# Dynamic convolution and SwiGLU: blocks 2 to 5 one at a time, with one queue of convolution steps, before the pairs begin

## The chip, the cores and the metric

One core of a Trainium2 chip. The metric is the time of one execution on the device in microseconds (us); shown is the median of several runs. The profile is one further execution, with the hardware profiler on. The engines are called PE (TensorE, matmuls), PEld (its weight loads), DVE (VectorE), ACT (ScalarE), POOL (GpSimd) and SP (SyncE, which issues the DMAs here). L301 is line 301 of the kernel before.

## The reference, cut to what matters

The input x is 4 x 4096 x 192. A causal convolution of 7 taps whose weights differ for every position and for each of 8 heads (24 channels a head) comes first, the weights through a softmax over the taps. Then a SwiGLU layer: RMS norm, two products with 192 x 1536 matrices, silu of the one times the other, and a product with a 1536 x 192 matrix.

```
w = exp(weight_gen - max over k); w = w / (sum over k + 1e-9)
x[b,s,h,:] = sum over k of w[b,s,h,k] * x_pad[b,s+k,h,:]
xn  = x / sqrt(mean(x*x) + 1e-6) * rms_g
out = (silu(xn @ w_gate) * (xn @ w_val)) @ w_out
```

The results are float32. The kernel gets there with float16 matmuls by splitting each operand into a high and a low float16 part.

## The kernel before, in words

The 16384 tokens are 32 **blocks** of 512 tokens (128 partitions x 4). Four blocks share one load of x and of the convolution's weights, a **group** (`load_x`, `load_w`; two buffers each). For each block i:

- **Convolution** (`conv`, L174): 13 steps on DVE, a product for each of the 7 taps (L193) and 6 additions (L204). A group's first block needs the group's softmax (`softmax`, L154), six steps on DVE and ACT.
- **Getting ready**: four squares with their sums on ACT (L209), the scale `rs` on DVE and its power -1/2 on POOL (L213, L217), the scaled block `xn` on DVE (L232), its float16 high part `sp` on ACT (L239), the low part on POOL (L241). Then `trans` (L249): SP issues a transposing DMA into `tt` (L253) and two copies with the halves swapped into `tu` (L256, L257). `tt` and `tu` have two buffers each.
- **Stage 1**: 12 chunks c of 128 hidden columns (`s1_mm`, L292). Each chunk is 18 matmuls into two PSUM banks, `pg` and `pv`; the first ones need `tt` alone, the others `tu`. The chunk is evacuated (`s1_evac`, L309) by a silu on ACT, `sg` (L314), and a product on DVE, `hf` (L316); then split (`s1_split`, L320) into the high part on ACT (L324) and the low part on POOL (L326), both in `hh`. The split runs two chunks behind, in the list `pend` (LAG = 2).
- **Stage 2**: the output product. For each of 4 tiles t of 128 tokens the 12 chunks are summed into one bank `po`, in 12 units of 4 chunks (`s2_mm`, L334; `unit`, L661). A finished tile is evacuated (`s2_evac`, L348) by ACT, `lo` (L353), and DVE, `ot` (L354); the fourth one sends the block out.

PSUM has eight banks, given out in turn (`ps1`).

The order on PE, DVE and ACT is written out by the program; POOL's and SP's in the main part is left to the framework. The start (the string START, run by `go`) brings in the weights and does blocks 0 and 1 whole, all of the convolution of block 2, and the first 4 of 13 steps for block 3 (LEAD). The main loop (L770) then takes blocks in **pairs** from block 2 on: stage 1 of block a, stage 1 of a + 1, stage 2 of a, stage 2 of a + 1.

Beside these stages run the steps that prepare later blocks. They wait in the list `work` as pairs of a cost and a function: 1.0 for a convolution step, 1.0 to 1.5 for a softmax step on DVE, 0.2 and 0.8 for `rs` and `xn`, and 0.0 for what is done on other engines. `begin` (L746) adds steps and sets a rate, at most 0.62 a slot in stage 1 and 0.88 in stage 2, and no more than spreads what is in the list over the stage's 24 slots. A slot is a chunk in stage 1 and a unit in stage 2. `beside` (L755) is called once a slot, behind that slot's matmuls and ahead of its evacuation: it adds the rate to an allowance and issues steps until the allowance is used up; steps of cost 0 follow at once. `first(a)` and `second(a)` (L632, L645) give the steps beside stage 1 and stage 2 of the pair a: `mix` (L593) gives convolution steps, `weigh` (L605) softmax steps, and `ready` (L616) what comes behind the last convolution step, with up to three steps of another list mixed in. If a block is not ready when its stage 1 is to be written out, the loop issues steps until it is (L773).

Of the kernel before, what the change touches and what calls it, by code (L numbers as in the profile page):

```python
# [20 lines left out]
J = 4  # L21
# [25 lines left out]
def tile_dynamic_conv_swiglu(  # L47
# [15 lines left out]
    NC = F // P  # L63
# [3 lines left out]
    SUB = R // J  # L67
    NB = NG * SUB
# [53 lines left out]
    def load_x(g):  # L122
        t0 = g * GT
        xt = p_x.tile([P, R + HALO, D], F32, tag="xg", name="xg")
        if t0 % S == 0:
            nc.vector.memset(xt[0:1, 0:HALO, :], 0.0)
            for a, b in ((1, 16), (16, P)):
                src = xf[t0 + a * R - HALO : t0 + b * R - HALO]
                nc.sync.dma_start(
                    out=xt[a:b, 0:HALO, :],  # L130
                    in_=src.rearrange("(p j) d -> p j d", j=R)[:, 0:HALO, :],
                )
        else:
            src = xf[t0 - HALO : t0 - HALO + GT]
            nc.sync.dma_start(
                out=xt[:, 0:HALO, :],
                in_=src.rearrange("(p j) d -> p j d", j=R)[:, 0:HALO, :],
            )
        xg[g] = xt
        load_x_slots(g, 0, J if g == 0 else R)  # L140

    def load_x_slots(g, a, b):
        src = xf[g * GT : (g + 1) * GT].rearrange("(p j) d -> p j d", j=R)
        nc.sync.dma_start(out=xg[g][:, HALO + a : HALO + b, :], in_=src[:, a:b, :])

    def load_w(g, a=0, b=R):
        if a == 0:
            wg[g] = p_w.tile([P, R, H, K], F32, tag="wt", name="wt")
        src = wf[g * GT : (g + 1) * GT].rearrange("(p j) c -> p j c", j=R)
        dst = wg[g].rearrange("p j h k -> p j (h k)")  # L150
        nc.sync.dma_start(out=dst[:, a:b, :], in_=src[:, a:b, :])
# [95 lines left out]
    xT = {}  # L247
# [44 lines left out]
    def s1_mm(i, c):  # L292
        f = slice(c * P, (c + 1) * P)
        pairs[i, c] = [ps1.tile([P, TB], F32, tag="pr", name=n) for n in ("pg", "pv")]
        orders = (OF_TT + OF_TU, OF_TU + OF_TT)
        for n in range(9):
            for m, pt in enumerate(pairs[i, c]):
                h = slice(m * L, (m + 1) * L)
                grp, wpart, xpart = orders[m][n]
                half, q = PLACE[grp, xpart]  # L300
                mm = nc.tensor.matmul(  # L301
                    pt, wm[h, grp, wpart, f], xT[i][half != m][h, q], start=(n == 0), stop=(n == 8)
                )
        return mm
# [4 lines left out]
    def s1_evac(i, c):  # L309
        pg, pv = pairs.pop((i, c))  # L310
        k = next(k for k, (a, b) in enumerate(SL) if a <= c < b)
        sg = p_e.tile([P, TB], F32, tag="sg", name="sg")
        o = 3 * k + 2 * SL[k][0]
        yield nc.scalar.activation(out=sg, in_=pg, func=AF.Silu, scale=isc[:, o : o + 1])  # L314
        hf_of[i, c] = p_e.tile([P, TB], F32, tag="hf", name="hf")
        yield nc.vector.scalar_tensor_tensor(  # L316
            out=hf_of[i, c], in0=pv, scalar=cs1[:, c : c + 1], in1=sg, op0=ALU.mult, op1=ALU.mult
        )

    def s1_split(i, c):  # L320
        if c == 0:
            hid[i] = p_h.tile([P, 2, NC, TB], F16, tag="hh", name="hh")
        hf = hf_of.pop((i, c))
        yield nc.scalar.activation(out=hid[i][:, 0, c, :], in_=hf, func=AF.Copy)  # L324
        low = nc.vector if i < 2 else nc.gpsimd
        yield low.tensor_tensor(  # L326
            out=hid[i][:, 1, c, :], in0=hf, in1=hid[i][:, 0, c, :], op=ALU.subtract
        )
# [5 lines left out]
    def s2_mm(i, t, c0, c1):  # L334
        if c0 == 0:
            po[i, t] = ps1.tile([P, 2 * D], F32, tag="pr", name="po")
        pt = po[i, t]
        c = slice(t * P, (t + 1) * P)
        for n in range(c0, c1):
            mm = nc.tensor.matmul(  # L340
                pt, hid[i][:, 0, n, c], wo[:, n, :], start=(n == 0), stop=False,
            )
            nc.tensor.matmul(  # L343
                pt[:, 0:D], hid[i][:, 1, n, c], wo[:, n, 0:D], start=False, stop=(n == NC - 1),
            )
        return mm

    def s2_evac(i, t):  # L348
        if t == 0:
            ot[i] = p_o.tile([P, J, D], F32, tag="ot", name="ot")  # L350
        pt = po.pop((i, t))
        lo = p_o.tile([P, D], F32, tag="lo", name="lo")
        yield nc.scalar.activation(out=lo, in_=pt[:, D:], func=AF.Identity, scale=so[:, 1:2])  # L353
        nc.vector.scalar_tensor_tensor(  # L354
            out=ot[i][:, t, :], in0=pt[:, 0:D], scalar=so[:, 1:2], in1=lo,
            op0=ALU.mult, op1=ALU.add,
        )
        g, s = divmod(i, SUB)
        if i == NB - 1:
            nc.sync.dma_start(out=outg[g, :, s * J + t, :], in_=ot[i][:, t, :])  # L360
        elif t == J - 1:
            nc.sync.dma_start(out=outg[g, :, s * J : (s + 1) * J, :], in_=ot.pop(i))
        yield
# [187 lines left out]
    def run(gen):  # L551
        for _ in gen:
            pass
# [39 lines left out]
    def mix(i, n):  # L593

        if i not in convs:
            convs[i] = conv(i)
        for _ in range(n):
            if begun.get(i, 0) < 2 * K - 1:
                begun[i] = begun.get(i, 0) + 1
                yield 1.0, lambda: next(convs[i])  # L600
# [4 lines left out]
    def weigh(g, steps):  # L605

        if g >= NG:
            return
        for n in steps:
            if n == 0:  # L610
                mixing[g] = softmax(g, 0, R)
            yield (1.0, 1.5, 0.0, 1.1, 1.3, 1.5)[n], lambda: next(mixing[g])
            if n == 5:
                yield 0.0, lambda: next(mixing[g], None)

    def ready(i, more):  # L616

        step = lambda: next(convs[i])
        for _ in range(J):
            yield 0.0, step  # L620
        for _ in range(2):
            yield from [x for x in [next(more, None)] if x]
        yield 0.2, step
        yield from [x for x in [next(more, None)] if x]
        yield 0.8, step
        for _ in range(2):
            yield 0.0, step
        yield 0.0, lambda: (next(convs[i], None), trans(i))

    whole = 2 * K - 1  # L630

    def first(a):  # L632

        if a == 2:
            more = weigh(1, range(6))
            yield from mix(3, whole)
            yield from ready(3, more)
            yield 0.0, lambda: (load_x(2), load_w(2))
            yield from more
        if a + 2 < NB:  # L640
            yield from mix(a + 2, whole)
        if a + 3 < NB:
            yield from mix(a + 3, EARLY)
# [15 lines left out]
    LAG = 2  # L659

    def unit(u):  # L661
        t, r = divmod(u, 3)
        return t, 4 * r, 4 * r + 4
# [74 lines left out]
    pend = []  # L738
# [3 lines left out]

    work, plan = [], [0.0, 0.0, 1.0]
    STAGE1, STAGE2 = 0.62, 0.88

    def begin(todo, slots, most):  # L746
        work.extend(todo)
        plan[:] = 0.0, 0.0, min(most, sum(cost for cost, _ in work) / slots)

    def do_next():  # L750
        cost, do = work.pop(0)
        do()
        plan[1] += cost

    def beside():  # L755
        plan[0] += plan[2]
        while work and (plan[1] < plan[0] or not work[0][0]):
            do_next()

    def stage2(i):  # L760
        for u in range(NC):
            s2_mm(i, *unit(u))
            beside()
            if u % 3 == 2:
                run(s2_evac(i, u // 3))

    with tc.manual_schedule(engines={
        mybir.EngineType.DVE, mybir.EngineType.PE, mybir.EngineType.Activation,
    }):
        for a in range(2, NB, 2):  # L770
            begin(first(a), 2 * NC, STAGE1)
            for i in (a, a + 1):
                while i not in xT:  # L773
                    do_next()
                for c in range(NC):
                    s1_mm(i, c)
                    if len(pend) == LAG:
                        run(s1_split(*pend.pop(0)))
                    beside()
                    run(s1_evac(i, c))  # L780
                    pend.append((i, c))
            while pend:
                run(s1_split(*pend.pop(0)))
            begin(second(a), 2 * NC, STAGE2)
            for i in (a, a + 1):
                stage2(i)
        assert not work
# [29 lines left out]
```

## Time and profile before

| | |
|---|---|
| median of 3 runs | 1233.79 us (1233.39 to 1234.16) |
| the profiled execution | 1235.56 us |
| its span, first to last instruction | 1233.8 us |
| mean granted clock of PE | 0.976 of full speed |
| busy: PE, DVE, ACT, POOL | 1171.5, 953.9, 659.8, 543.1 us |

How to read it: busy time is the time in which an engine had an instruction running. Matmuls are pipelined, so that a busy PE need not be at its peak. Shares over the whole span are averages of unlike stages; the stretch from 142 to 338 us is the one that the rows below look at.

### The profile page before, as it was taken

The numbers are of one execution on the slowest core, as the hardware profiler recorded it, in microseconds if no ns is written. First come the engines' busy times: TensorE is split into PE (matmuls) and PEld (weight loads), VectorE is DVE, ScalarE is ACT, GpSimd is POOL, SyncE is SP. The second block draws the span as 40 slices with busy tenths as digits, with TensorE's granted clock in tenths as the row PEclk, the third lists the DMA queues.
The fourth block names the chain that finished last, engine by engine and source line by source line (L and its number), as shares of the span: only waits on it lengthen the run. The fifth ranks groups of instructions, "written<-read, shape, count | busy, mean of one in ns | idle before, by whom it ended". The sixth has DMA issues, their size and how long they took to land.

```text
span 1233.8 us, 24345 instructions
## 1 busy us (share of the span) xinstructions
PE 1171.5 (95%) x10124; PEld 640.0 (52%) x10124; DVE 953.9 (77%) x1157; ACT 659.8 (53%) x1304; POOL 543.1 (44%) x460
## 2 busy tenths in 40 slices
PE   5899687969999999999999999999999999999998
PEld 3446235426455564645546464655546464554646
DVE  6998738559787888778887888878887889878531
ACT  4893642433654646465563646455563646556362
POOL 1100432343453636455463636456363645546351
PEclk8999889879899999999999999999999999999999
DMA  8602301011403040210503041110502011020300
GB/s 213 163 8 82 131 22 30 23 27 27 137 2 78 2 137 27 40 39 7 158 1 78 1 121 43 28 52 1 163 1 52 26 40 40 6 73 1 78 1 27
DMA packets 68086, 67.34 MB, mean 55 GB/s; under 512 B 52492, under 2 KB 55052, under 8 KB 67080
## 3 DMA queue, kind: packets, MB, share of 16 engines
q1 hardware_dynamic: 66872, 63.43, 19.2%
q10 hardware_dynamic: 1040, 2.36, 0.7%
q8 instruction: 79, 1.29, 0.4%
q14 instruction: 31, 0.25, 0.1%
q0 software_dynamic: 64, 0.00, 0.0%
HBM read 28.03 MB, written 12.58 MB: 33 GB/s over the span
## 4 chain that ended last, share of the span: by engine, by line
PE 83%; DVE 4%; issue 4%; DMA 3%; ACT 3%; POOL 2%; SPq 0%; POOLq 0%; ACTq 0%; DVEq 0%
PE pg L301 53%; PE po L340 17%; PE po L343 8%; PE pv L301 5%; DMA tt<-sp 1%; DMA tu<-tt 1%; DVE tmp L193 1%; DMA rawa<-in_moe_w_gate_dram 1%; DVE acc L204 1%; POOL hh L326 1%; POOL sp L241 1%; POOL rs L217 1%; ACT sg L314 1%; ACT junk L209 1%; DVE hf L316 0%
## 5 line engine op out<-in xcount | busy, mean ns | idle before, releaser
L301 PEld LDWEIGHTS <-wm 64*128 64x128 f16 x6912 | 348.1, 95 | 455.6 <-DMA tt<-sp 35.8
L326 POOL TENSOR_TENSOR hh<-hf,hh 128x512 f16<-128x512 f32 x360 | 446.1, 1245 | 312.3 <-ACT hh L324 312.2
L301 PE MATMUL pg<-tt,wm 64*128 64x512 f16 x1920 | 484.6, 381 | 34.6 <-DMA tt<-sp 34.3
L301 PE MATMUL pv<-tu,wm 64*128 64x512 f16 x1920 | 483.0, 380 | 4.3 <-DMA tu<-tt 4.3
L316 DVE SCALAR_TENSOR_TENSOR hf<-pv,cs,sg 128x512 f32<-128x512 f32 x384 | 284.0, 744 | 164.3 <-ACT sg L314 164.0
L301 PE MATMUL pv<-tt,wm 64*128 64x512 f16 x1536 | 399.7, 381 | 2.8 <-DVE hf L316 1.0
L314 ACT ACTIVATE sg<-pg,isc 128x512 f32<-128x512 f32 x384 | 262.6, 685 | 259.1 <-PE pv L301 246.5
L301 PE MATMUL pg<-tu,wm 64*128 64x512 f16 x1536 | 398.0, 380 | 0.6 <-DMA tu<-tt 0.6
L340 PE MATMUL po<-wo,hh 128*128 128x384 f16 x1536 | 377.9, 326 | 0.0
L343 PE MATMUL po<-wo,hh 128*128 128x192 f16 x1536 | 376.3, 246 | 0.0
L193 DVE TENSOR_TENSOR tmp<-xg,wt 128x768 f32<-128x768 f32 x194 | 257.1, 1327 | 1.8 <-DMA xg<-in_x_dram 1.8
L324 ACT ACTIVATE hh<-hf 128x512 f16<-128x512 f32 x384 | 238.6, 622 | 33.0 <-DVE hf L316 32.9
L204 DVE TENSOR_TENSOR acc<-acc,tmp 128x768 f32<-128x768 f32 x180 | 234.5, 1303 | 1.1
L340 PEld LDWEIGHTS <-hh 128*128 128x128 f16 x1536 | 150.3, 98 | 105.4 <-issue 7.2
L217 POOL TENSOR_TENSOR rs<-rs,mhalf 128x4 f32<-128x4 f32 x32 | 41.9, 1308 | 253.2 <-DVE rs L213 253.1
L343 PEld LDWEIGHTS <-hh 128*128 128x128 f16 x1536 | 150.3, 98 | 0.0
L354 DVE SCALAR_TENSOR_TENSOR ot<-po,so,lo 128x192 f32<-128x192 f32 x128 | 52.2, 409 | 75.8 <-ACT lo L353 75.8
L353 ACT ACTIVATE lo<-po,so 128x192 f32<-128x192 f32 x128 | 51.1, 411 | 108.2 <-PE po L343 105.1
L209 ACT ACTIVATE junk<-acc 128x192 bf16<-128x192 f32 x128 | 46.0, 359 | 69.6 <-DVE acc L204 61.8
L241 POOL TENSOR_TENSOR sp<-xn,sp 128x768 f16<-128x768 f32 x29 | 48.4, 1669 | 58.7 <-ACT sp L239 58.7
L239 ACT ACTIVATE sp<-xn 128x768 f16<-128x768 f32 x30 | 25.3, 843 | 84.7 <-DVE xn L232 84.6
L232 DVE TENSOR_TENSOR xn<-acc,rs 128x768 f32<-128x768 f32 x30 | 28.7, 956 | 21.8 <-POOL rs L217 21.8
(83 smaller groups left out, 316.3 us busy)
## 6 DMA issues: line engine op xcount, KB each, us to landing
tu<-tt SPq DMA_DIRECT2D x64, 192.0 KB, 2.9
out_dram<-ot SPq DMA_DIRECT2D x31, 384.0 KB, 3.3
xg<-in_x_dram SPq DMA_DIRECT2D x7, 1536.0 KB, 9.1
wt<-in_weight_gen_dram SPq DMA_DIRECT2D x7, 448.0 KB, 9.6
wost<-in_moe_w_out_dram SPq DMA_DIRECT2D x1, 2304.0 KB, 8.9
xg<-in_x_dram SPq DMA_DIRECT2D x4, 576.0 KB, 5.9
xg<-in_x_dram SPq DMA_DIRECT2D x4, 504.0 KB, 5.2
rawa<-in_moe_w_val_dram ACTq DMA_DIRECT2D x2, 384.0 KB, 7.8
```

Of the source, the lines that this page charges most:

```text
L193: yield nc.vector.tensor_tensor(out=dst.rearrange("p j (h c) -> p (j h) c", h=H), in0=xk, in1=wk, op=ALU.mult)
L204: yield nc.vector.tensor_tensor(out=acc, in0=acc, in1=dst, op=ALU.add)
L209: yield nc.scalar.activation(out=junk, in_=acc[:, j - a, :], func=AF.Square, accum_out=ssq[:, j : j + 1])
L217: yield nc.gpsimd.tensor_tensor(out=rs, in0=rs, in1=mhalf, op=ALU.pow)
L241: yield low.tensor_tensor(out=sp[:, :, D:], in0=xn, in1=sp[:, :, 0:D], op=ALU.subtract)
L301: mm = nc.tensor.matmul(pt, wm[h, grp, wpart, f], xT[i][half != m][h, q], start=(n == 0), stop=(n == 8))
L314: yield nc.scalar.activation(out=sg, in_=pg, func=AF.Silu, scale=isc[:, o : o + 1])
L316: yield nc.vector.scalar_tensor_tensor(out=hf_of[i, c], in0=pv, scalar=cs1[:, c : c + 1], in1=sg, op0=ALU.mult, op1=ALU.mult)
L324: yield nc.scalar.activation(out=hid[i][:, 0, c, :], in_=hf, func=AF.Copy)
L326: yield low.tensor_tensor(out=hid[i][:, 1, c, :], in0=hf, in1=hid[i][:, 0, c, :], op=ALU.subtract)
L340: mm = nc.tensor.matmul(pt, hid[i][:, 0, n, c], wo[:, n, :], start=(n == 0), stop=False,)
L343: nc.tensor.matmul(pt[:, 0:D], hid[i][:, 1, n, c], wo[:, n, 0:D], start=False, stop=(n == NC - 1),)
```

## The change

Blocks 2 to 5 are taken singly: stage 1 of a block and then its stage 2 at once. Pairs begin with block 6. For the single blocks one queue, `early(7)`, holds all the steps for blocks 3 to 7 and the loads of groups 2 and 3 in order; it is never refilled, and its rate is fixed at 0.75 a slot in stage 1 and 0.88 in stage 2. Where the next block's convolution can begin, up to five of its steps are offered to `ready` as the mixed-in list. A bare block number in the queue is a mark: `beside` stops there, and lets the unused allowance go, until stage 1 of that block has been written out (`past`); it stands ahead of `ready` of block i with the number i - 2, the block whose `tt` and `tu` are used again. `early` takes up what `first(2)` did for block 3. In the single blocks, stage 2 goes by thirds of the hidden columns: units 1 to 4 are chunks 0 to 3 of tiles 0 to 3, units 5 to 8 chunks 4 to 7, units 9 to 12 chunks 8 to 11, so that four banks `po` are open together and all four tiles are evacuated in the last four units. The last two splits of stage 1 are no longer run ahead of stage 2, but behind its first two units.

```diff
@@ -629,14 +629,28 @@
 
     whole = 2 * K - 1
 
+    past = set()
+
+    def early(last):
+
+        more = weigh(1, range(6))
+        for i in range(3, last + 1):
+            yield from mix(i, whole)
+            if i > 3:
+                yield 0.0, i - 2
+            g, s = divmod(i - 3, SUB)
+            if s == 0:
+                yield from ready(i, more)
+                yield 0.0, lambda g=g: (load_x(g + 2), load_w(g + 2))
+                yield from more
+                more = weigh(g + 2, range(6))
+            else:
+                ahead = mix(i + 1, 5) if i < last else iter(())
+                yield from ready(i, ahead)
+                yield from ahead
+
     def first(a):
 
-        if a == 2:
-            more = weigh(1, range(6))
-            yield from mix(3, whole)
-            yield from ready(3, more)
-            yield 0.0, lambda: (load_x(2), load_w(2))
-            yield from more
         if a + 2 < NB:
             yield from mix(a + 2, whole)
         if a + 3 < NB:
@@ -742,6 +756,7 @@
 
     work, plan = [], [0.0, 0.0, 1.0]
     STAGE1, STAGE2 = 0.62, 0.88
+    SOLO, RATE = 6, (0.75, 0.88)
 
     def begin(todo, slots, most):
         work.extend(todo)
@@ -755,30 +770,52 @@
     def beside():
         plan[0] += plan[2]
         while work and (plan[1] < plan[0] or not work[0][0]):
+            if isinstance(work[0][1], int):
+                if work[0][1] not in past:
+                    plan[1] = max(plan[:2])
+                    break
+                work.pop(0)
+                continue
             do_next()
 
-    def stage2(i):
+    def stage1(i):
+        while i not in xT:
+            if isinstance(work[0][1], int):
+                work.pop(0)
+            else:
+                do_next()
+        for c in range(NC):
+            s1_mm(i, c)
+            if len(pend) == LAG:
+                run(s1_split(*pend.pop(0)))
+            beside()
+            run(s1_evac(i, c))
+            pend.append((i, c))
+        past.add(i)
+
+    def stage2(i, turn=False):
         for u in range(NC):
-            s2_mm(i, *unit(u))
+            t, c0, c1 = (u % J, u // J * 4, u // J * 4 + 4) if turn else unit(u)
+            s2_mm(i, t, c0, c1)
+            if pend:
+                run(s1_split(*pend.pop(0)))
             beside()
-            if u % 3 == 2:
-                run(s2_evac(i, u // 3))
+            if c1 == NC:
+                run(s2_evac(i, t))
 
     with tc.manual_schedule(engines={
         mybir.EngineType.DVE, mybir.EngineType.PE, mybir.EngineType.Activation,
     }):
-        for a in range(2, NB, 2):
+        begin(early(SOLO + 1), 1, STAGE1)
+        for i in range(2, SOLO):
+            plan[2] = RATE[0]
+            stage1(i)
+            plan[2] = RATE[1]
+            stage2(i, True)
+        for a in range(SOLO, NB, 2):
             begin(first(a), 2 * NC, STAGE1)
             for i in (a, a + 1):
-                while i not in xT:
-                    do_next()
-                for c in range(NC):
-                    s1_mm(i, c)
-                    if len(pend) == LAG:
-                        run(s1_split(*pend.pop(0)))
-                    beside()
-                    run(s1_evac(i, c))
-                    pend.append((i, c))
+                stage1(i)
             while pend:
                 run(s1_split(*pend.pop(0)))
             begin(second(a), 2 * NC, STAGE2)
```

## Rows read from the trace of the kernel before

**Rows 1.** The page: busy us (share) and instructions of PE; its clock in 40 slices.
```profile
PE 1171.5 (95%) x10124; PEld 640.0 (52%) x10124; DVE 953.9 (77%) x1157; ACT 659.8 (53%) x1304; POOL 543.1 (44%) x460
...
PEclk8999889879899999999999999999999999999999
```

**Rows 2.** Waits of PE from 119 to 340: us in total, times, longest.
```profile
PE pg L301 <- DMA tt<-sp: 34.3, 4, 13.6
PE pv L301 <- DMA tu<-tt: 4.3, 4, 1.8
```

**Rows 3.** Windows by stage: length, busy PE, PEld, DVE, ACT, POOL; clock, DMA, GB/s.
```profile
119.00:142.40 23.40, 23.40 (x218) 10.43 (x216) 17.18 (x19) 13.16 (x22) 10.88 (x10) 1.00 0.31 111
142.40:160.20 17.80, 2.41 (x11) 0.57 (x10) 7.17 (x8) 7.39 (x14) 4.44 (x4) 0.64 0.64 192
160.20:185.00 24.80, 24.76 (x209) 11.63 (x209) 11.02 (x14) 13.31 (x23) 12.26 (x11) 0.92 0.00 1
185.00:208.50 23.50, 23.48 (x192) 17.15 (x190) 21.79 (x28) 6.43 (x18) 4.61 (x4) 1.00 0.05 18
...
219.90:245.00 25.10, 25.07 (x206) 11.93 (x205) 15.12 (x15) 12.51 (x26) 9.25 (x8) 0.88 0.00 1
...
260.00:284.00 24.00, 23.92 (x207) 11.64 (x207) 17.15 (x17) 13.26 (x22) 12.09 (x11) 0.93 0.01 1
...
307.70:312.60 4.90, 1.83 (x10) 0.51 (x11) 4.69 (x8) 2.60 (x10) 0.00 (x0) 0.84 0.47 111
312.60:337.60 25.00, 24.96 (x208) 11.93 (x209) 17.39 (x20) 16.62 (x25) 13.63 (x12) 0.89 0.48 148
```

**Rows 4.** The chain of waits from 142 to 162: start, us, what.
```profile
147.71 1.02 POOL rs L217
...
148.75 0.97 DVE xn L232
...
149.74 0.85 ACT sp L239
...
150.66 1.64 POOL sp L241
...
152.32 3.71 DMA tt<-sp
...
156.09 4.10 DMA tu<-tt
```

**Rows 5.** DVE by line and form, stage 2 from 185 to 208.5: count, busy, mean ns.
```profile
L193 DVE TENSOR_TENSOR tmp<-xg,wt 128x768 f32<-128x768 f32 x8 | 7.6, 950 | 0.0
```

**Rows 6.** The same for DVE in stage 1 of block 5, 260 to 284.
```profile
L316 DVE SCALAR_TENSOR_TENSOR hf<-pv,cs,sg 128x512 f32<-128x512 f32 x11 | 8.2, 744 | 13.3 <-ACT sg L314 13.3
L204 DVE TENSOR_TENSOR acc<-acc,tmp 128x768 f32<-128x768 f32 x3 | 5.5, 1826 | 0.0
L193 DVE TENSOR_TENSOR tmp<-xg,wt 128x768 f32<-128x768 f32 x3 | 4.6, 1529 | 0.0
```

**Rows 7.** The same for POOL, 260 to 284.
```profile
L326 POOL TENSOR_TENSOR hh<-hf,hh 128x512 f16<-128x512 f32 x11 | 12.7, 1156 | 17.3 <-ACT hh L324 17.3
```

**Rows 8.** The same for ACT and DVE before block 3, 142.4 to 160.2.
```profile
L209 ACT ACTIVATE junk<-acc 128x192 bf16<-128x192 f32 x4 | 1.5, 363 | 2.3 <-DVE acc L204 2.2
...
L209 ACT ACTIVATION_READ_ACCUMULATOR junk<-acc 128x1 f32 x4 | 0.7, 186 | 0.0
...
L159 DVE TENSOR_TENSOR wt<-wt,mx 128x896 f32<-128x896 f32 x1 | 1.1, 1091 | 0.0
```

**Rows 9.** The page's costliest groups, the silu on ACT over the whole span.
```profile
L314 ACT ACTIVATE sg<-pg,isc 128x512 f32<-128x512 f32 x384 | 262.6, 685 | 259.1 <-PE pv L301 246.5
```

**Rows 10.** The chain of waits before block 4: issue of a copy, the second copy.
```profile
216.38 0.47 SPq L256
216.90 2.99 DMA tu<-tt
```

**Rows 11.** SP's issues, 513 to 520: the second copy of block 12.
```profile
519.05 0.59 SPq L257 DMA_DIRECT2D tu<-tt  x1
```

## The prediction

> **What bounds the kernel now.** I read the page first. PE is busy for 95% of the span, and the line of its clock shows dips in the first third only [rows 1]: what can be won lies there, or in less PE work. The change leaves every matmul in place, so only the holes count. The waits of PE name them: 34.3 us in four waits for the transposed block `tt`, 4.3 for the swapped copy `tu` [rows 2]. The windows by stage then show where they lie [rows 3]. Let S1(i) be stage 1 of block i, S2(i) its stage 2. At full clock S1 takes 23.4 us (first row of [rows 3]); S2 of two blocks takes 23.5, so 11.75 each. S1(2) ends at 142.4, and PE then does 2.4 us of work in 17.8 until block 3's copy lands at 160.2. The same happens before blocks 4 (until 219.9), 5 (260.0) and 6 (312.6), and after each hole S1 takes 24.0 to 25.1 instead of 23.4, because the granted clock is 0.88 to 0.93: it fell to the lower level (1.2 GHz) in the hole and came back some microseconds into the stage. From 142.4 to the end of S1(6) at 337.6 are 195.2 us; the work in them is four S1 and four S2, 4 x 23.4 + 4 x 11.75 = 140.6. **54.6 us are lost**, all in this stretch.
>
> Why block 3 is late is in the chain of waits [rows 4]: after the last convolution step come the squares, `rs` on POOL at 147.71, `xn`, `sp`, its low half on POOL, the transpose (3.71), the copy (4.10). Without the squares this is 12.5 us, with them some 15, in which PE has nothing: S1(3) is next in its order, and S2(2), whose input is complete, stands behind it.
>
> **The change, part by part.**
>
> *Order of the blocks.* With blocks 2 to 5 run singly, S2(i) stands between S1(i) and S1(i+1): 11.75 us of PE work lie where the chain of block i+1 runs. No instruction of PE is added.
>
> *Thirds.* S2 goes through c = 0..3 of all four tiles first, then 4..7, then 8..11. So it needs the last splits of S1, which are now issued behind S2's slots 1 and 2, only in its slot 9, 8 x 0.98 = 7.8 us in. Four sums are open instead of one; they take the four PSUM banks that c = 8 and 9 left, evacuated 2 slots before. Cost nothing; the cover is those 7.8 us. If the last split (of c = 11, on POOL) came later than that, PE would wait for it.
>
> *Queue.* I counted it by hand: 12 slots at 0.75 and 12 at 0.88 are 19.56 units per block. Of block 3's 13 steps 4 are done in the start; the 9 left go into slots 1-3, 5-7, 9-11 of S1(2), where the old rate of 0.62 placed 8 and the rest came behind. The marks (a block's number as a queue entry) are always passed when they are reached, as S1(i-2) lies far back.
>
> *DVE beside S1.* A conv step takes 0.95 us with POOL quiet [rows 5]; in S1 1.83 and 1.53 [rows 6], for POOL's 1.16 us products [rows 7] lie beside it. Mean 1.68. Four slots of 1.95 us then hold 3 steps and 4 `hf`: 3 x 1.68 + 4 x 0.74 = 8.0 against 7.8. DVE is at its limit, 0.2 late per four slots; four pairs of PSUM banks let it be about two slots late before PE waits. I take 0, the upper end is below. On the same rows: the Trainium skill, page "SBUF — State Buffer", section "Who interferes with whom", says that VectorE and GpSimd share a port pair as an exclusive lock and the loser is blocked for a whole instruction; the trace agrees (0.95 against up to 1.83), and it speaks against raising the rate.
>
> *Block 3.* Slot 10 of S1(2) ends at 142.4 - 2 x 1.95 = 138.5, its `hf` 1.5 later, 0.7 more for the steps before: step 9 runs from 140.7 to 142.2. ACT's order has four squares here, 1.5 + 0.7 = 2.2 [rows 8], ahead of slot 11's `sg`: 144.4. Then `sg` (0.69 [rows 9]) and `hf` (0.74) of slots 11 and 12 overlap to 146.7. The new order puts two softmax steps on DVE before `rs`: 1.1 to 147.8, the second (1.09 [rows 8]) waits for a POOL product until 148.9, so 150.0. With the durations of [rows 4]: `rs` 1.2 to 151.2, `xn` 152.1, `sp` 153.0, low half 154.7, `tt` 158.4. The copy: the second is issued 0.5 after the first and lands 2.99 later [rows 10], 3.5, so **162.0** (160.2 before: later, by the squares and the softmax). PE has done S2(2) by 154.2. S1(3) ends 24.8 after the copy, as in [rows 3]: 186.8. The loads of group 2 need only the last read of `xg`, two slots earlier, so I put nothing for them; if SP had them in front of the copy, that is rival 2.
>
> *Block 4.* Its steps fill slots 9-12 of S2(2) and 2-4, 6-8, 10-12 of S1(3), the last in the last slot: `hf` of slot 11 at 186.7, step to 188.1, squares 190.3, `sg` and `hf` of slot 12 to 191.7. Before `rs` the queue puts two steps of block 5, each behind one of POOL's last two products: 195.5. `rs` and its power behind the next step: 197.5; then `xn` 198.4, `sp` 199.3, low half 201.0, `tt` 204.8, `tu` **208.3**. S2(3) ended at 198.6. S1(4) ends 25.1 later [rows 3], 233.4.
>
> *Block 5.* Five of its steps run ahead, nine are done in S2(3), the last in slot 5 of S1(4); `xn` has slot 10, at 229.0. With a wait for POOL 230.9, `sp` 231.8, low half 234.0, `tt` 237.8, `tu` 241.3. S2(4) ends at 233.4 + 11.75 = 245.2: 3.9 to spare, **no hole**. The squares in slot 5 hold that slot's `hf` back by some 3.5 us, within the banks' reach. Block 6 has `xn` in slot 3 of S1(5), block 7 its transpose in slot 8 of S2(5): no hole. So S1(6) ends at 245.2 + 35.15 + 23.4 = 303.7.
>
> *Pairs from block 6.* The queue is empty there, so the pairs run as now with a clearer start.
>
> **Sum.** Lost up to S1(4)'s end: 233.4 - 142.4 - 2 x 35.15 = 20.7, afterwards 0. Against 54.6 the gain is 33.9 (337.6 - 303.7). The profiled execution took 1235.56 with a span of 1233.8; it stands 1.8 over the median 1233.79. So 1201.7 in its own terms, 1199.9 for the median. Ends for the unknown: if POOL's products stay out of the way of both chains, block 3 is 3 and block 4 some 4 us earlier, 1193; if every step in S1 of the chains takes 1.83, 4 later plus 2 of clock, 1206.
>
> **Rivals.**
> 1. DVE sets the pace of S1. If each step sits out a whole product, 0.95 + 1.16 = 2.11, four slots take 3 x 2.11 + 4 x 0.74 = 9.3: 1.5 late, 4.5 a block, 18 in four blocks if the banks absorb none: 1218; half absorbed, 1209. The Trainium skill's page above makes this the worst case. Against it: the mean in [rows 6] is 1.68. Chance 0.08.
> 2. Block 5 is late all the same, or block 3's copy stands behind the group's loads on SP: 4 to 6 us past its need plus 1.7 of clock (25.1 - 23.4), 1206 to 1208. For it: only 3.9 to spare. Chance 0.10.
> 3. The marks hold the queue, so the change does less than it says: each of blocks 5 to 7 keeps a hole like block 4's, 208.3 - 198.6 = 9.7 less 2 us done on `tt`: 3 x 8 more, 1224. Against it: my count. Chance 0.03.
> 4. Slower: the pairs lose their lead. Before block 12 the second copy is issued at 519.05 [rows 11] and lands 2.99 later at 522.0, where S1(12) starts at about 524.8 (337.6 + 46.8 + 2 x 70.2): 2.8 to spare. If a new phase made it 3 us late at all 12 pair starts from block 8 on, with 1.7 of clock each, that is 12 x 4.7 = 56: 1256. It decides from 2.8 us per pair start on. Against it: the pairs' code is unchanged and their queue starts emptier. Chance 0.03.
> 5. No change to be seen: the new holes eat the gain, 17 us longer each. Nothing speaks for it. 0.02.
>
> **Numbers.** Forecast 0.72 (1194 to 1206); shorter chains, 1186 to 1194, 0.02; rivals as above. 1193 to 1211 holds the forecast, rival 2 and a little of 1: 0.72 + 0.10 + 0.03, some 0.85; I leave it there because both ends of the chains' bounds lie in it. About 0.2% is what a measurement can tell from no change. Faster by more 0.95, within it 0.02, slower 0.03.
>
> **What would show it.** Right: PE's waits for `tt` and `tu` fall from four to two of each, before S1(3) and S1(4), with `tu` near 162 and 208; DVE's `hf` less than two slots late; S1(6) ends near 304; nothing new after it. Wrong: a wait of PE for `hf`, or for the low half of `hh` inside S2; a third hole before block 5; transposes of the pairs nearer to PE's start than now.

## The result, and the profile after

The changed kernel takes 1203.7 us (median of 4 runs) against 1233.6 before: 29.9 us less, a ratio of 0.977 (95% interval 0.974 to 0.980). The forecast was 1199.9, and a range of 1193 to 1211. The profiled execution took 1203.92 with a span of 1202.1. Runs differ by one to two microseconds in where stage 1 of block 2 starts (118.15 here, 119.02 before, up to 119.98 below), a difference from the start of the program that the change does not touch; stages are therefore counted from that point.

On the page after, PE is busy for 97% of the span (1165.0 us). Its clock in 40 slices, as in [rows 1]:

```profile
PEclk9999988999999999999999999999999999999999
```

The waits of PE after, from 119 to 340, as in [rows 2] (us in total, times, longest):

```profile
PE pg L301 <- DMA tt<-sp: 10.0, 2, 6.4
PE pv L301 <- DVE ot L354: 2.2, 2, 1.9
PE pv L301 <- DMA tu<-tt: 1.9, 2, 1.4
PE po L343 <- POOL hh L326: 0.8, 1, 0.8
PE pg L301 <- DMA tu<-tt: 0.4, 2, 0.2
PE po L340 <- ACT sg L314: 0.3, 1, 0.3
```

Two holes are left, as forecast, and the waits for `tt` fall from 34.3 to 10.0 us. But there are three waits that were not there before, for `ot`, for the low half of `hh` and for `sg`. The windows by stage, as in [rows 3] (length, busy PE, PEld, DVE, ACT, POOL; clock, DMA, GB/s), say where. In order: S1(2), S2(2), the hole, S1(3) from the copy's landing, S2(3), the hole, S1(4), S2(4), S1(5), S2(5), S1(6):

```profile
118.15:141.56 23.41, 23.41 (x217) 10.43 (x217) 18.68 (x19) 12.38 (x22) 10.42 (x9) 1.00 0.37 119
141.56:153.40 11.84, 11.84 (x98) 8.57 (x96) 7.97 (x9) 7.91 (x17) 6.04 (x5) 1.00 0.57 207
153.40:160.58 7.18, 2.01 (x12) 0.65 (x11) 6.91 (x10) 2.12 (x3) 0.00 (x0) 0.82 0.50 110
160.58:185.03 24.45, 24.45 (x207) 11.74 (x206) 18.80 (x19) 12.73 (x21) 10.91 (x10) 0.91 0.05 17
185.03:196.80 11.77, 11.77 (x98) 8.56 (x96) 8.25 (x9) 4.05 (x12) 5.27 (x4) 1.00 0.01 2
196.80:206.92 10.12, 3.03 (x12) 0.83 (x11) 8.46 (x11) 1.71 (x5) 2.40 (x1) 0.61 0.44 102
206.92:232.08 25.16, 25.16 (x206) 11.85 (x206) 15.13 (x17) 11.71 (x25) 12.15 (x9) 0.89 0.02 7
232.08:245.38 13.30, 12.20 (x98) 8.52 (x98) 11.39 (x11) 5.18 (x9) 8.34 (x6) 1.00 0.29 60
245.38:271.52 26.14, 23.97 (x218) 11.85 (x217) 22.33 (x29) 15.81 (x34) 15.40 (x11) 1.00 0.18 46
271.52:283.38 11.86, 11.86 (x97) 8.56 (x97) 10.67 (x11) 5.69 (x14) 8.14 (x5) 1.00 0.41 143
283.38:306.90 23.52, 23.47 (x216) 11.83 (x217) 20.70 (x28) 16.52 (x28) 15.84 (x11) 1.00 0.30 92
```

S2(2) and S2(3) take their plain length right behind their S1. The holes end at 160.6 and 206.9; with the 0.9 us by which this execution started earlier, the forecast of 162.0 and 208.3 was off by 0.5 each. There is no hole before blocks 5 and 6. Counted from the start of S1(2), block 3's copy lands at 42.4 us, against 41.2 before: it comes no earlier, and the hole before block 3 is shorter by the work of S2(2) that now lies ahead of it. Block 4's copy lands at 88.8 instead of 100.9, so there the queue counts as well as the order of the blocks; no run takes the two apart. What the forecast does not have is in two stages: S2(4) takes 13.30 instead of 11.75, S1(5) 26.14 instead of 23.4, at full clock. From the end of S1(2) to the end of S1(6) it is 165.3 us against 195.2 before: 29.9 gained where 33.9 were worked out.

The chain that makes block 3 ready, as in [rows 4], from the timelines of DVE, POOL and SP: the second softmax step, the power, `xn`, the low half, the transpose, the second copy, without the lines between them (start, length, engine, line; in brackets the idle time before, and who ended it).

```profile
146.59 1.97 DVE L159 TENSOR_TENSOR wt<-wt,mx 128x896 f32<-128x896 f32 x1
148.72 1.01 POOL L217 TENSOR_TENSOR rs<-rs,mhalf 128x4 f32<-128x4 f32 x1 [1.11 <-DVE rs L213]
149.76 0.96 DVE L232 TENSOR_TENSOR xn<-acc,rs 128x768 f32<-128x768 f32 x1 [1.12 <-POOL rs L217]
151.68 1.64 POOL L241 TENSOR_TENSOR sp<-xn,sp 128x768 f16<-128x768 f32 x1 [1.95 <-ACT sp L239]
153.34 1.45 SPq L253 DMA_TRANSPOSE tt<-sp  x1
157.58 0.59 SPq L257 DMA_DIRECT2D tu<-tt  x1
```

The softmax step that lies ahead of `rs` takes 1.97 us here, against 1.09 with POOL quiet [rows 8]: it ends 0.95 us after POOL's last product (147.61), as assumed. SP issues nothing between the transpose and the copies, so no load of the group stood in their way. DVE in S1(3) and POOL in S1(3), as in [rows 6, 7]:

```profile
L316 DVE SCALAR_TENSOR_TENSOR hf<-pv,cs,sg 128x512 f32<-128x512 f32 x11 | 8.2, 744 | 5.8 <-ACT sg L314 5.8
L193 DVE TENSOR_TENSOR tmp<-xg,wt 128x768 f32<-128x768 f32 x4 | 6.5, 1624 | 0.0
L204 DVE TENSOR_TENSOR acc<-acc,tmp 128x768 f32<-128x768 f32 x4 | 5.5, 1372 | 0.0
```
```profile
L326 POOL TENSOR_TENSOR hh<-hf,hh 128x512 f16<-128x512 f32 x10 | 11.6, 1156 | 20.8 <-ACT hh L324 20.8
```

A step takes 1.50 on the mean, less than the 1.68 at the lower rate: some of the steps start when a product is half done and wait for its rest alone (1.37 us for the step at 169.53, beside a product from 168.92 to 170.08). DVE still waits 5.8 us for `sg`, so it is not the pace, and S1(2) took its plain 23.41 at the rate of 0.75. The pairs kept their lead. The second copy of block 12 after, as in [rows 11], and the first matmul of S1(12) in the kernel before:

```profile
487.47 0.59 SPq L257 DMA_DIRECT2D tu<-tt  x1
```
```profile
526.52 0.39 PE L301 MATMUL pg<-tt,wm 64*128 64x512 f16 x1
```

With the 2.99 of [rows 10] the copy lands at 490.5; S1(12) starts at 494.9, so 4.4 us are to spare. Before it was 4.5 (526.5 - 522.0), not 2.8: the prediction had put the start at about 524.8.

Why S2(4) and S1(5) are longer is to be read on ACT. Two of its waits from 232 to 255 (us in total, times, longest):

```profile
ACT junk L209 <- DVE acc L204: 5.9, 1, 5.9
ACT sp L239 <- DVE xn L232: 4.5, 1, 4.5
```

ACT did its instructions in the order in which the program wrote them. The queue put `sp` of block 5 ahead of slot 10's `sg`; `sp` waits for `xn`, `xn` for the power on POOL, and that lies behind two of POOL's products. ACT stood 4.5 us, from 228.5 to 233.0, while the chunks of slots 10 to 12 came to wait. The last splits of block 4 came late, and PE waited in S2(4), 0.3 us for a PSUM bank that `sg` had not yet read and 0.8 for the last low half. In S2(4) the squares of block 6 then stood 5.9 us for DVE's last step, ahead of three `lo`; the `ot` that follow were late, and PE waited 1.9 us for a PSUM bank in S1(5). That was the theory for the experiments; the rival was that DVE and POOL, shutting each other out at the higher rate, are simply too slow.

### The profile page after: what moved, and what is told of

Same layout as the page of the kernel before. It is cut to its first block, busy times and chain, and to the rows that moved or that the text cites. A ratio compares the mean times of both kernels' runs of the same rounds, so it can differ in the third digit from the quotient of the medians.

```text
span 1202.1 us, 24340 instructions
## 1 busy us (share of the span) xinstructions
PE 1165.0 (97%) x10124; PEld 637.1 (53%) x10124; DVE 957.2 (80%) x1157; ACT 658.0 (55%) x1304; POOL 552.4 (46%) x460
## 4 chain that ended last, share of the span: by engine, by line
PE 76%; POOL 2%; DVE 2%; issue 1%; ACT 1%; POOLq 0%
PE pg L301 46%; PE po L340 17%; PE po L343 9%; PE pv L301 4%; POOL hh L326 2%; DVE tmp L193 1%; DVE acc L204 0%; DVE xn L232 0%; DVE ot L354 0%; DVE hf L316 0%; POOL rs L217 0%; ACT junk L209 0%; ACT sp L239 0%; POOL sp L241 0%; ACT sg L314 0%
## 5 line engine op out<-in xcount | busy, mean ns | idle before, releaser
L326 POOL TENSOR_TENSOR hh<-hf,hh 128x512 f16<-128x512 f32 x360 | 456.0, 1275 | 299.6 <-ACT hh L324 299.6
L193 DVE TENSOR_TENSOR tmp<-xg,wt 128x768 f32<-128x768 f32 x194 | 262.3, 1355 | 2.7 <-DMA xg<-in_x_dram 2.7
L217 POOL TENSOR_TENSOR rs<-rs,mhalf 128x4 f32<-128x4 f32 x32 | 41.2, 1288 | 226.2 <-DVE rs L213 226.2
```

The lines of the kernel that those rows point to most:

```text
L193: yield nc.vector.tensor_tensor(out=dst.rearrange("p j (h c) -> p (j h) c", h=H), in0=xk, in1=wk, op=ALU.mult)
L326: yield low.tensor_tensor(out=hid[i][:, 1, c, :], in0=hf, in1=hid[i][:, 0, c, :], op=ALU.subtract)
```

## The experiments

Eight kernels, each the changed kernel with an edit. The times beside each other are medians; lengths come from the profiles. The changed kernel takes 165.2 us from the start of S1(2) to that of S1(6) (118.15 to 283.38).

**ACT's order.** `ready` takes the numbers of mixed-in steps ahead of the squares, ahead of `rs`, ahead of `xn` and ahead of `sp` from a table; (0, 2, 1, 0) is what it did.

```diff
+    MIXED = {5: (1, 0, 1, 1), 6: (3, 1, 1, 1)}
...
     def ready(i, more):
         step = lambda: next(convs[i])
+        n0, n1, n2, n3 = MIXED.get(i, (0, 2, 1, 0))
+        take = lambda n: (x for _ in range(n) for x in [next(more, None)] if x)
+        yield from take(n0)
         for _ in range(J):
             yield 0.0, step
-        for _ in range(2):
-            yield from [x for x in [next(more, None)] if x]
+        yield from take(n1)
         yield 0.2, step
-        yield from [x for x in [next(more, None)] if x]
+        yield from take(n2)
         yield 0.8, step
+        yield from take(n3)
```

> The rates stay; only places in the queue change: the squares of block 5 come one slot later, its xn one slot earlier and its sp a slot behind xn, and the squares of block 6 wait until stage 1 of block 5. Theory (ACT stands at squares and sp that wait for DVE and POOL, ahead of evacuations that are ready): stage 2 of block 4 falls from 13.3 to about 12, stage 1 of block 5 from 26.1 to about 24; 1199 to 1201 us. Rival (POOL and DVE shutting each other out at this rate): both stages stay within 0.5 us, 1203.7.

Measured: 1201.39 (before, in the same set of runs, 1233.31; ratio 0.974, 0.972 to 0.976), 2.3 less than the changed kernel by the medians and just above the range that was expected. PE's waits from 119 to 340, then S2(4) and S1(5) in the windows, then, of ACT's waits from 208 to 245, the one for `xn`:

```profile
PE pg L301 <- DMA tt<-sp: 10.0, 2, 6.4
PE pv L301 <- DMA tu<-tt: 2.0, 2, 1.5
PE pg L301 <- DMA tu<-tt: 0.4, 2, 0.2
```
```profile
233.22:245.08 11.86, 11.86 (x98) 8.61 (x96) 11.76 (x11) 2.73 (x6) 7.61 (x5) 1.00 0.40 68
245.08:268.50 23.42, 23.42 (x217) 10.44 (x217) 21.04 (x28) 15.86 (x32) 16.96 (x11) 1.00 0.20 52
```
```profile
ACT sp L239 <- DVE xn L232: 1.5, 1, 1.5
```

Both stages are back at their plain length and only the waits for the DMAs are left: 161.3 us to S1(6), 3.9 less in the profiles. The wait for `acc` ahead of the squares, 5.9 us above, is gone. The rates are the same, and POOL is no faster. Its products in S2(4), in the changed kernel and here:

```profile
L326 POOL TENSOR_TENSOR hh<-hf,hh 128x512 f16<-128x512 f32 x5 | 7.8, 1582 | 0.0
```
```profile
L326 POOL TENSOR_TENSOR hh<-hf,hh 128x512 f16<-128x512 f32 x4 | 7.4, 1887 | 0.0
```

So DVE and POOL do shut each other out (1156 ns in S1(3) above), even more than in the changed kernel, and still PE no longer waits: new places in the queue were enough. In the changed kernel the five products took 0.4 us each more than in S1(3), on the same chain behind ACT; how much of PE's 0.8 us is theirs was not measured apart. The edit also has `rs` ready at 226.4 and its power at once behind it, at 226.5, where in the changed kernel the power waited from 228.2 to 230.1 behind two of POOL's products; so ACT's wait for `xn` falls from 4.5 to 1.5, and not only the place of `sp` counts.

**The chains of the two holes.** The same table, for other blocks (the rest of the edit as above):

```diff
+    MIXED = {3: (0, 0, 0, 0), 4: (0, 0, 0, 0)}
```

> Blocks 3 and 4 get ready with nothing mixed in: two softmax steps and three steps of block 5 are issued behind xn instead of ahead of it. Theory (the two holes left end with a chain on which these steps lie): the copy for block 3 lands 2 to 3 us earlier than 160.6, the one for block 4 another 3 to 4, in all 5 to 7 us less, 1197 to 1199. Rival (POOL's last products or the transposing DMA end the chain, and the steps lie beside them): within 1 us of 1203.7.

Measured: 1197.4 (ratio 0.971, 0.969 to 0.972), 6.3 less than the changed kernel. Counted from the start of S1(2), the copy for block 3 lands at about 40.3 instead of 42.4 (157.31 + 2.99 - 119.98), the one for block 4 at 82.7 instead of 88.8. The windows S2(2), S1(3), S2(3) with what is left of the hole, S1(4), S1(5):

```profile
143.39:159.85 16.46, 13.71 (x98) 9.43 (x97) 11.47 (x14) 8.03 (x17) 6.89 (x5) 0.90 0.61 194
159.85:183.27 23.42, 23.42 (x218) 10.44 (x217) 21.84 (x25) 14.88 (x24) 10.94 (x10) 1.00 0.05 18
183.27:202.66 19.39, 14.28 (x109) 9.32 (x107) 15.48 (x18) 5.82 (x16) 6.24 (x5) 0.92 0.19 42
202.66:226.89 24.23, 24.23 (x206) 11.67 (x206) 16.28 (x19) 11.71 (x25) 12.15 (x9) 0.92 0.05 17
240.21:267.58 27.37, 25.47 (x217) 12.47 (x217) 23.56 (x31) 16.34 (x34) 16.63 (x11) 0.94 0.17 44
```

The mixed-in steps did lie on the chain that ends both holes. The price is a later last split of block 2, for which PE now waits 2.7 us inside S2(2); that wait lies where the hole was. S1(3) then starts at the full clock.

**Both edits together.**

```diff
+    MIXED = {3: (0, 0, 0, 0), 4: (0, 0, 0, 0), 5: (1, 0, 1, 1), 6: (3, 1, 1, 1)}
```

> The two edits together: blocks 3 and 4 get ready with nothing mixed in, and the squares, xn and sp of blocks 5 and 6 have the later places. From the start of stage 1 of block 2 to that of block 6 the changed kernel takes 165.2 us, with the first edit 159.5, with the second 161.3. Theory (two separate losses, the chains of the two holes and ACT's order after them): the sum, and the 1.2 us more that the first edit had in stage 1 of block 5 go as well: 154 to 155 us, 1192 to 1194 for the whole. Rival (the second edit only moved a wait that returns when blocks come earlier): 158 to 160, 1197.

Measured: 1192.48 (ratio 0.967, 0.966 to 0.968), and 154.3 us to S1(6) (118.02 to 272.33). That is 10.9 less than the changed kernel, where the two edits alone gave 5.8 and 3.9: the two losses are separate and add up, and the 1.2 us that S1(5) had lost more with the edit of the chains alone (27.37 against 26.14) go as well.

**The thirds undone.**

```diff
-            stage2(i, True)
+            stage2(i)
```

> The thirds are undone: stage 2 of the single blocks goes tile by tile again, so its third unit needs the last split. Theory (the thirds only cover the last splits, and where PE stands before block 3 or 4 anyway that cover is worth nothing): stage 2 of blocks 2 and 3 grows by 3.5 to 5 us, but the copies for blocks 3 and 4 land at 160.6 and 206.9 as in the changed kernel, so nothing is lost there; stage 2 of block 4 grows from 13.3 to about 19, that of block 5 from 11.9 to about 16, and the wait of 1.9 us for ot in stage 1 of block 5 goes: in all 6 to 9 us more, 1210 to 1213 us. Rival (the thirds carry the gain in all four blocks): 4 to 5 us in each, 1220 to 1224. Second rival (they do nothing): 1203.7.

Measured: 1209.28 (ratio 0.982, 0.979 to 0.984), 5.6 more than the changed kernel by the medians; 168.7 us to S1(6), 3.5 more. S2(3), S1(4) from the copy's landing, S2(4), S2(5):

```profile
184.21:203.28 19.07, 15.07 (x98) 9.78 (x97) 14.19 (x17) 5.65 (x15) 6.85 (x5) 0.82 0.17 22
206.35:228.69 22.34, 22.34 (x206) 11.62 (x205) 15.13 (x17) 11.72 (x25) 12.16 (x9) 1.00 0.01 6
228.69:250.68 21.99, 16.05 (x98) 9.87 (x97) 16.68 (x19) 7.03 (x16) 8.33 (x6) 0.77 0.17 37
274.10:287.74 13.64, 12.21 (x99) 8.47 (x98) 11.76 (x14) 7.78 (x17) 6.74 (x5) 1.00 0.52 190
```

S2(4) and S2(5) grow by 8.7 and 1.8: that is what the cover for the last splits is worth where no hole follows. S1(5), which has no wait for `ot` here, gets 2.7 back (23.42). In S2(2) and S2(3) the longer stage lies in the hole. That the whole is still less than the 6 to 9 us expected was not foreseen: S1(4) takes 22.34 from the landing instead of 25.16, and S1(3) 22.34 instead of 24.45. PE waited in pieces with matmuls between them; the granted clock fell inside S2(3), to 0.82 over the stage, and was back at the full level when S1(4) began. The two starts together gave 4.9 us back.

**Thirds for blocks 4 and 5 alone**, to have that by itself:

```diff
-            stage2(i, True)
+            stage2(i, i > 3)
```

> Stage 2 of blocks 2 and 3 goes tile by tile, that of blocks 4 and 5 by thirds. Theory (PE stands for the copy of blocks 3 and 4 in any case; where it stands inside stage 2, matmuls lie between the waits and stage 1 of the next block starts at the full clock): the copies land as in the changed kernel, stage 1 behind them takes 22.3 us from the copy's landing instead of 24.5 and 25.2, the clock of these stages is 1.00: 4 to 5 us less, 1198.5 to 1200. Rival (the clock falls wherever PE waits some microseconds, and the full clock seen with all four blocks tile by tile came from there): 1203.7.

Measured: 1202.69 (ratio 0.974, 0.972 to 0.976), 164.1 us to S1(6): 1.2 less, not 4 to 5. S1(3), S1(4), S1(5):

```profile
162.49:184.82 22.33, 22.33 (x206) 11.53 (x205) 18.80 (x19) 12.74 (x21) 10.93 (x10) 1.00 0.05 19
207.44:231.09 23.65, 23.65 (x207) 11.46 (x206) 15.12 (x17) 11.72 (x25) 12.15 (x9) 0.94 0.02 6
244.40:271.78 27.38, 25.48 (x218) 12.39 (x217) 23.57 (x31) 16.34 (x34) 16.64 (x11) 0.94 0.17 44
```

The starts are faster, by 2.1 and 1.5 us. But the copies land 0.5 and 0.7 later behind their stage 1, and S1(5) has the same wait of 1.9 us for `ot` with 27.38 instead of 26.14, at a clock of 0.94 instead of 1.00. The faster starts are there; what they are worth in the whole is within the spread of the runs.

**The old rate beside stage 1.**

```diff
-    SOLO, RATE = 6, (0.75, 0.88)
+    SOLO, RATE = 6, (0.62, 0.88)
```

> The rate beside stage 1 of the single blocks is 0.62 again. Theory (the higher rate is needed to have block 5 ready in time; the 4.2 us that stage 2 of block 4 and stage 1 of block 5 lose come from the order on ACT): the copies for blocks 3 and 4 land within 1.5 us of the changed kernel's, block 5 has a hole of 3 to 5 us and a start at half clock, some of the 4.2 us come back: 1203 to 1209. Rival (at 0.75 DVE is the pace, being shut out by POOL): the 4.2 us come back and no hole opens, 1199 to 1200.

Measured: 1217.03 (ratio 0.986, 0.985 to 0.988), 13.3 more, beyond both theories. Blocks 3 and 4 are indeed ready as early as in the changed kernel (the copies land at 41.9 and 86.8 from S1(2)'s start, instead of 42.4 and 88.8). Block 5 is not: a hole of 5.4 us with its restart, and S1(6) starts 3.9 later (169.1). The expectation stopped there. The queue is never refilled, and at 0.62 it falls behind: softmax steps and block 7's steps from `rs` to the transpose are left when the pairs begin. They come out beside S1(6), `sp` of block 7 (at 301.38) ahead of slot 3's `sg` (303.53) on ACT, and PE waits for a bank. The wait, and the window from the start of S1(6) to the end of S1(7), 52.80 instead of 47.1:

```profile
PE pg L301 <- ACT sg L314: 2.4, 1, 2.4
```
```profile
288.61:341.41 52.80, 49.24 (x434) 23.59 (x433) 39.28 (x47) 33.67 (x60) 28.19 (x24) 0.97 0.23 73
```

The later start of S1(6) and this stretch make 9.5 of the 12.7 us between the two profiled spans. So with four single blocks the rate of 0.75 is needed for blocks 5 to 7, not for 3 and 4.

**Pairs from block 4.**

```diff
-    SOLO, RATE = 6, (0.75, 0.88)
+    SOLO, RATE = 4, (0.75, 0.88)
```

> Only blocks 2 and 3 are single, pairs begin with block 4. Theory (a single block is worth its stage 2 as a cover for the next block's chain; blocks 2 and 3 had the two longest holes, and before block 5 a hole returns): a hole of 5 to 8 us and a half-clock start before block 5, against it the 4.2 us in stage 2 of block 4 and stage 1 of block 5 go: 2 to 6 us more than the changed kernel, 1206 to 1210. Rival (each of the four single blocks carries about a quarter of the gain): 1218. Second rival (blocks 4 and 5 singly bring nothing or harm): 1200 to 1203.7.

Measured: 1203.62 (ratio 0.976, 0.975 to 0.978), the same as the changed kernel. The theory fell, and the second rival holds: singles for blocks 4 and 5 add nothing. PE's waits from 119 to 340:

```profile
PE pg L301 <- DMA tt<-sp: 9.9, 2, 6.4
PE pv L301 <- DMA tu<-tt: 2.5, 3, 1.5
PE pg L301 <- DMA tu<-tt: 1.7, 4, 0.9
```

The hole before block 5 is 1.9 us (two waits for `tu`) and not 5 to 8: its steps stand first in the queue, and with no steps of block 6 mixed in (the queue ends with block 5) its transpose is issued at 228.3 instead of 235.6. The 4.3 us of S2(4) and S1(5) are not there either. 163.8 us to S1(6), 1.5 less; S1(6) then waits 0.9 for its copy, which takes back a part. The edit takes the single order, the thirds and the rate from blocks 4 and 5 at once, and the time stays: the whole gain is that of blocks 2 and 3 with their queue.

**The best of these.** Both edits of the queue, and stage 2 of block 3 alone tile by tile:

```diff
+    MIXED = {3: (0, 0, 0, 0), 4: (0, 0, 0, 0), 5: (1, 0, 1, 1), 6: (3, 1, 1, 1)}
...
-            stage2(i, True)
+            stage2(i, i != 3)
```

> Both edits of the queue, and stage 2 of block 3 alone goes tile by tile. Theory: before block 3 the first edit left no hole at full length, before block 4 a hole with a start at clock 0.92 (24.2 us from landing); that start goes to 22.3: 1.5 to 2 us less than both edits alone, 1190 to 1192. Rival (the last split of block 3 now ends stage 2 later than the copy lands): 0 to 3 us more than both edits alone.

Measured: 1191.41 (ratio 0.967, 0.964 to 0.969), 12.3 less than the changed kernel and 42.1 less than the kernel before. Against both edits alone it is 1.1 less by the medians, which their spread can't tell, and 0.7 in the profiles (153.6 against 154.3), not 1.5 to 2. S2(3) and S1(4):

```profile
181.57:201.19 19.62, 14.89 (x99) 9.79 (x98) 15.21 (x17) 5.54 (x15) 5.60 (x5) 0.83 0.20 41
201.19:224.60 23.41, 23.41 (x217) 10.43 (x217) 18.97 (x22) 15.42 (x31) 13.59 (x10) 1.00 0.05 18
```

No wait for a DMA is left between blocks 2 and 6; PE waits 7.5 us inside S2(2) and S2(3) for the last splits.

## Why the prediction was right, and the term that was mis-sized

- **What bounds it, and the cover.** Right. The 54.6 us were holes before four blocks, and stage 2 of the block before covers the chain. After: 24.7 lost (165.3 - 140.6), where 20.7 were worked out.
- **Blocks 3 and 4.** Right to 0.5 us each, with the squares, the softmax steps, the two steps ahead of `rs` and POOL's products on the chain. That the mixed-in steps lie on it was argued there, and the edit of the chains showed it: 2.1 and another 4.0 us. For the squares and the products the traces alone speak.
- **The price of a restart.** The prediction set S1 behind a hole against 23.4 and took 1.7 us (25.1 - 23.4) in rivals 2 and 4. But some 12 of its matmuls are done in the hole; the others take 22.3 at the full clock (the thirds undone), so the restart costs up to 2.8. The sum is not touched by it, for it uses the whole lengths of [rows 3].
- **Block 5 without a hole** (rival 2). Right, with less to spare: its second copy was issued at 239.83 and landed 2.99 later at 242.8, 2.6 us ahead of S1(5). The forecast had 3.9.
- **The step that failed** is the cost of 0 for the evacuations behind block 5's and block 6's preparation ("within the banks' reach" for the squares, nothing for `sp`, nothing for block 6's squares in S2(4)). It measured 1.55 in S2(4) and 2.74 in S1(5), 4.3 together; as S1(4) ended 0.5 earlier than forecast, counted from the end of S1(2), and the two stages behind are 0.2 longer, this is the whole difference between 29.9 and 33.9. One of the prediction's own signs of being wrong is in the trace: PE's wait of 0.8 us for the low half of `hh` in S2(4). And `hf` of slot 10 of S1(4) came 6.3 us behind its matmuls, over three slots, where less than two were to be the sign of being right. The squares in slot 5 alone were costed, and `xn` with one wait for POOL; what the engine behind them does was not followed. Three chunks' `sg` stood behind `sp`, and three `lo` behind block 6's squares. The edit of the places in the queue took both away.
- **DVE's limit** (rival 1). It did not set the pace: at the same rate the waits went with new places in the queue. In S1(3) DVE's steps took 1.62 and 1.37 us against 0.95 with POOL quiet [rows 5], and POOL's product its 1.16; in S2(4), beside steps that follow each other, the product took 1.58 to 1.89. The Trainium skill, page "SBUF — State Buffer", section "Who interferes with whom", says that a DVE instruction with two SBUF inputs contends with a GpSimd instruction that reads SBUF, over a shared port pair that is an exclusive lock; the trace agrees, on both sides.
- **The marks** (rival 3). They never hold: when the queue is paid out as the program does it, none is reached before its stage 1 has been written out, so that without them the steps come in the same order. This is worked out from the program; no run left them out.
- **The thirds.** They were to cover the last splits of all four blocks at no cost. They do so for blocks 4 and 5 (8.7 and 1.8 us when undone). For blocks 2 and 3 they brought nothing in this kernel, since the copy ended the hole either way, and the start of the next stage 1 was slower with them.
- **Singles for blocks 4 and 5.** The forecast gave them the holes before blocks 5 and 6 and their slow starts, 15.0 + 0.6 + 4.9 + 1.6, some 22 of the 54.6 us lost [rows 3]. The edit of the pairs showed that pairs from block 4 on do as well: once blocks 3 and 4 come with the new queue, block 5's steps are early enough either way. The sum was right for the change as a whole, but that part of it is not owed to single blocks.
- **The pairs** (rival 4) kept their lead: 4.4 us after, 4.5 before.

## What to carry to other kernels

When PE waits for a preparation chain, look for finished work that stands behind the waiting instruction in the written order, and put that work ahead of it; then shorten the chain itself by taking off it whatever another engine's queue put there. A step placed in an in-order engine's list costs not its own time but the time until its operands are there, for everything behind it: ask of every moved step what it waits for at that point and who stands behind it. Where a queue is paid out at a fixed rate, the rate must also empty it before the next scheme takes over.

## What the hardware showed that was not expected

Behind a hole of 7 and of 10 us, stage 1 took 24.45 and 25.16 us from the copy's landing, at a clock of 0.91 and 0.89; the same matmuls took 22.34 at the full clock in the kernel without thirds. So the restart cost 2.1 and 2.8 us. Waits cut into pieces by matmuls let the clock fall too (4.0 us of waits and a clock of 0.82 in S2(3) of the kernel without thirds). But the slow stretch then lay in stage 2, which for blocks 2 and 3 had time until the copy landed, and in five of the six stages 2 tile by tile in which this happened (blocks 2 to 4 of the kernel without thirds, blocks 2 and 3 of the one with thirds for blocks 4 and 5, block 3 of the last) the next stage 1 ran at the full clock; in the sixth, block 3 of the kernel with thirds for blocks 4 and 5, it had 0.94. A single wait of 1.9 us in S1(5) left the clock at 1.00 in one kernel (26.14 us) and was followed by 0.94 in two others (27.37, 27.38), with the same matmuls: a short wait may or may not bring the clock down, and the runs do not say what decides.
